# Seven block products for the gate, token scales computed one stage earlier, and gated tiles in older tiles' homes

## The chip, the cores and the metric

The kernel runs on one core of a Trainium2 chip. The time is the device time of that core for one launch, in microseconds (us). Three runs of the kernel before took 1465.34, 1465.96 and 1466.18 us; their median is 1465.96 us. The core has a matmul engine (TensorE, PE in the profile, with its weight loads in a row of their own, PEld), three engines for elementwise work (VectorE is DVE, ScalarE is ACT, GpSimd is POOL) and an engine that only issues transfers here (SyncE, SP). Each engine works through its own queue in order; semaphores tie the queues together.

## The reference

The inputs have 8 batches of 576 tokens, 4608 in all, with 8 heads of 64 features (512 features a token). Three stages follow one another. The first is an attention by 32 landmarks per head. The second transforms its output x by a real Fourier transform over tokens and features, normalizes, and runs a feed-forward pair. The third is a gated feed-forward with a shift by one token:

```
u = x + real(fft(fft(x, axis=1), axis=2));  un = normalize(u)
y = u + relu(un @ w_ch1) @ w_ch2                      # 512 -> 2048 -> 512
y_prev = y shifted by one token inside its batch (zeros at the first)
xk = mu_k * y + (1 - mu_k) * y_prev
xr = mu_r * y + (1 - mu_r) * y_prev
k  = relu(xk @ w_k);  v = (k * k) @ w_v               # 512 -> 1024 -> 512
out = sigmoid(xr @ w_r) * v                           # w_r is 512 x 512
```

## The kernel before

The 4608 tokens are cut into 9 blocks of 512. Every product of the two feed-forward stages is taken in 16-bit halves: each operand is a high and a low part, and three matmuls (high by high, high by low, low by high, the list `PARTS`) make one product. The attention and the transform of the 8 batches run beside the first blocks of the feed-forward stage. Then come, for each block, a half block `first` of the hidden layer (function `first`, results in banks `ph`) and the second layer (`second`, results in banks `acc`).

Matrices can be multiplied in 2 by 2 blocks with seven products in place of eight. `first` of the feed-forward stage does so from block 3 on, and `first` of the gated stage does so for `w_k`: the operand is turned into seven sums and differences of its blocks (`split` in `prep`, 128 by 512 elements each), the weights likewise (`pair` in the background), and the seven products of 12 matmuls with 256 columns are added up in two banks, with copies by ScalarE and additions by VectorE in between. The gate, `xr @ w_r`, is taken plainly before: `gate(j)` makes 12 matmuls with 512 columns for each of four token groups, in a bank `gp` of its own, and one Sigmoid.

`prep(i)` makes the operands of gated block i. It loads the block and the token before it (`yb`), squares the four feature quarters on ScalarE, adds them on GpSimd, transposes and sums them (`token_sums`: 4 transposes and a reduction), turns the sum of each token into powers of two (`r`, `nz`, `qi`), spreads `r` over the partitions (`spread`: 4 transposes into a bank), copies that to `rs`, and then, for each quarter and each of the two mixes, runs one ScalarE and two VectorE instructions (`mixed`). `xk` is split into seven parts, `xr` into four, each with one ScalarE copy (high part) and one GpSimd subtraction (low part).

What is recorded is put in order by a planner (`Plan.issue`, with costs from `Engine.cost` and a priority `lead`), except the matmuls with `chain=True`: these keep the order in which the program records them. `fillers` lays that order: between the steps of `first` stand one or two pieces of the previous half block's `second` and of the gate. So TensorE's order is fixed by hand, and the other engines' by the planner.

Of the eight banks, `acc` holds 0 to 3 and `ph` 4 and 5; everything named `gp` shares the last two. Memory is cut into pools: `com` lives throughout; `pa` (with `ub`, `w2`, `uc`, `un` and `w1`) ends with the feed-forward stage, and what is in `pb2` (for blocks 1 to 8 everything that `prep` makes, `k2`, `sg`, the second half of `w_v`) starts only when the last use of anything in `pa` is over. `pb` starts when the attention's pools are done.

In the profile L190 is the recorder of every VectorE, ScalarE and GpSimd instruction, L335 is `mm`, L351 is `tr` (transposes) and L319 is every transfer. So the tile names tell the operations apart: `gp<-w_r,xr` is the gate, `ph<-xk,w_k` the hidden layer, `acc<-w_v,k` the second layer of the gated stage, `rm` a product's copy, `k` a square of the hidden layer (`k2` in the code).

Of the kernel before, what the change touches and what calls it, by code (L numbers as in the profile page):

```python
# [23 lines left out]
DM = H * D  # L24
# [172 lines left out]
class Plan:  # L197
# [28 lines left out]
    def tile(self, pool, shape, dt, name, tag=None, bufs=1):  # L226
# [12 lines left out]
        return Ref(t, view)  # L239

# [829 lines left out]
def build(nc, tc, a):  # L1070
# [5 lines left out]
    with stack, tc.manual_schedule():  # L1076
# [53 lines left out]
        def rows_of(name, r, g):  # L1130
# [3 lines left out]
            "w_k": [128, 2, 7, 2, FF2 // 2], "w_r": [128, 2, 4, DM],  # L1134
# [24 lines left out]
        def w2_room():  # L1159
            return iss.tile(pa, [128, 2, 4, DM], F16, "w2", bufs=3)  # L1160
# [7 lines left out]
        far_pairs = [far_pair("w_k", c, g) for g in range(2) for c in range(2)]  # L1168
        far_items = [
            (rows_of("w_v", r, 0), kept[f"w_v{r // 4}"][:, :, r % 4]) for r in range(8)  # L1170
        ] + [(rows_of("w_r", r, 0), kept["w_r"][:, :, r]) for r in range(4)]
# [131 lines left out]

        ORDER = [4 * g + f for g in range(4) for f in (2, 3, 0, 1)]
# [16 lines left out]
        def copy(ps, func=AF.Copy):  # L1321
            t = room()
            s_.activation(t, ps, func)
            return t

        class Block:
# [78 lines left out]
            def second(self, f, half):  # L1405
# [21 lines left out]
                for m in (2 * half, 2 * half + 1):  # L1427
# [3 lines left out]
                    iss.load(ys[:, m, BLK * self.i:BLK * self.i + BLK], u[m])  # L1431

# [6 lines left out]
        more = iss.place(pa, [128, 2, 2 * WCH + 2], I32, "more", "ub_2")  # L1439
# [85 lines left out]
        for n in ("w_k", "w_r", "w_v0"):  # L1525
            fetch(pb, n)
# [7 lines left out]
        fetch(pb2, "w_v1")  # L1534

        def prep(i):
            iss.lead = SOON
            pool, nb = (pb2, 2) if i else (pb, 1)
# [6 lines left out]
            q = None  # L1545
            for c in range(0, 4, 2):
                pair = []
                for d in (c, c + 1):
                    pair.append(
                        iss.tile(com, [128, BLK + 1], F32, "sq", "h", 3) if i  # L1550
                        else iss.tile(pool, [128, BLK + 1], F32, "sq", bufs=3)
                    )
                    s_.activation(pair[-1], y[:, d], AF.Square)
                g_.tensor_tensor(pair[1], pair[0], pair[1], op=ALU.add)
                if q is not None:
                    g_.tensor_tensor(pair[1], pair[1], q, op=ALU.add)
                q = pair[1]
            o = D * i
            s2 = tmp("s2")
            g_.tensor_tensor(s2, q[:, 1:], q[:, 0:BLK], op=ALU.add)  # L1560
            if i < B:
                g_.tensor_copy(s2[:, o:o + 1], q[:, o + 1:o + 2])
            ss = token_sums(s2)
            ex = small().bitcast(I32)
            v_.tensor_scalar(
                ex, ss.bitcast(I32), 24, None, op0=ALU.logical_shift_right
            )
            r, ri = small(), small()
            v_.tensor_scalar(r.bitcast(I32), ex, -1, 196, op0=ALU.mult, op1=ALU.add)
            v_.tensor_scalar(  # L1570
                r.bitcast(I32), r.bitcast(I32), 23, None, op0=ALU.logical_shift_left
            )
            v_.tensor_scalar(ri.bitcast(I32), ex, 58, None, op0=ALU.add)
            v_.tensor_scalar(
                ri.bitcast(I32), ri.bitcast(I32), 23, None, op0=ALU.logical_shift_left
            )
            nz, qi = [iss.tile(com, [128, 4], F32, n, bufs=3) for n in ("nz", "qi")]
            v_.tensor_scalar(nz, ri, 1.0 / WS, None, op0=ALU.mult)
            v_.scalar_tensor_tensor(qi, ri, 0.25, ri, op0=ALU.mult, op1=ALU.mult)
            rb = spread(r)  # L1580
# [147 lines left out]
        def fillers(n):  # L1728
# [6 lines left out]
            if i == NB:  # L1735
                return late
# [109 lines left out]
```

## Time and profile before

| What | Value |
|---|---|
| median of three runs | 1465.96 us |
| the profiled execution, device time | 1466.6 us |
| its span, first to last instruction | 1464.8 us |
| TensorE busy | 1441.8 us (98%) |
| VectorE, ScalarE, GpSimd busy | 995.1, 695.9, 368.4 us (68%, 48%, 25%) |
| mean granted clock of TensorE | 0.994 of full speed |
| gated stage, first `ph<-xk,w_k` to last `acc<-w_v,k` | 999.4 to 1460.2 us |

The page's chain of work that ended last is 95% TensorE. A matmul's busy time there overlaps its neighbour's, so its mean in the grouped lines (379 ns for 512 columns) is a latency and not what one more of it costs; what one costs is read from the chain of work, where a run of x12 or x24 matmuls has the time it took from start to next start. Idle time of VectorE, ScalarE and GpSimd counts only where TensorE waits for them.

### The profile page before, as it was taken

The page shows a single profiled execution, that of the slowest core. Times are in us where ns is not written, and L with a number is a line of the kernel's source. Part 1 is how long each engine was busy: PE and PEld are TensorE (multiplying, and loading weights), DVE is VectorE, ACT ScalarE, POOL GpSimd, SP SyncE. Part 2 cuts the span into 40 slices and gives each one's busy share as a digit, 9 for nine tenths or more (in the row PEclk, how much of TensorE's full clock was granted, in tenths as well). Part 3 has the DMA queues.
Part 4 walks back from the last instruction along what each step waited for, and adds up shares of the span by engine and source line. Part 5 has one row for each costly group of instructions (what it writes and reads, how often), then busy time and mean ns, then how long its engine had stood idle before and what let it go on. Part 6 is the DMA issues. An engine that isn't in the chain of part 4 may idle for free.

```text
span 1464.8 us, 25189 instructions
## 1 busy us (share of the span) xinstructions
PE 1441.8 (98%) x10016; PEld 878.7 (60%) x10016; DVE 995.1 (68%) x1976; ACT 695.9 (48%) x1430; POOL 368.4 (25%) x429
## 2 busy tenths in 40 slices
PE   9889999999999999999999999999899999999998
PEld 5445445554566676666666666666566666666664
DVE  7877685765865786776767685324687788768762
ACT  4776544454453444454554533224545545454531
POOL 3012123232320123031022121001434434353410
PEclk9989999999999999999999999999999999999999
DMA  8695663634735545555466663412001110101000
GB/s 309 203 333 201 218 216 101 233 134 151 251 128 190 202 153 184 200 195 179 145 220 239 260 221 131 158 59 87 29 30 58 37 51 29 58 30 55 34 30 29
DMA packets 76790, 211.40 MB, mean 144 GB/s; under 512 B 6400, under 2 KB 31232, under 8 KB 66816
## 3 DMA queue, kind: packets, MB, share of 16 engines
q1 hardware_dynamic: 76672, 209.78, 40.8%
q8 instruction: 79, 1.29, 0.4%
q14 instruction: 39, 0.32, 0.1%
HBM read 168.34 MB, written 41.42 MB: 143 GB/s over the span
## 4 chain that ended last, share of the span: by engine, by line
PE 95%; DVE 3%; ACT 1%; DMA 0%; POOL 0%; issue 0%; DVEq 0%; ACTq 0%; POOLq 0%
PE acc L335 38%; PE ph L335 35%; PE gp L335 18%; PE gp L351 3%; PE spare L1122 1%; DVE uc L190 0%; DMA more<-in_w_ch 0%; DVE un L190 0%; DVE small L190 0%; POOL xk L190 0%; DVE A L190 0%; ACT Y L190 0%; DVE mx L190 0%; DVE w L190 0%; DVE cst L190 0%
## 5 line engine op out<-in xcount | busy, mean ns | idle before, releaser
L335 PEld LDWEIGHTS <-w 128*128 128x128 f16 x4320 | 417.7, 99 | 298.7 <-issue 41.7
L335 PE MATMUL acc<-h,w 128*128 128x512 f16 x1728 | 429.2, 380 | 3.3 <-DVE A L190 3.3
L335 PE MATMUL ph<-un,w 128*128 128x256 f16 (+1 forms) x2592 | 405.1, 298 | 3.5 <-DVE un L190 1.9
L190 DVE TENSOR_TENSOR rm<-ph,rm 128x512 f32<-128x512 f32 x126 | 86.9, 689 | 184.9 <-ACT rm L190 130.9
L335 PE MATMUL acc<-w_v,k 128*128 128x512 f16 x864 | 199.2, 380 | 0.0
L335 PE MATMUL ph<-xk,w_k 128*128 128x256 f16 x1512 | 184.1, 275 | 5.0 <-POOL xk L190 2.2
L190 ACT ACTIVATE rm<-ph 128x512 f32<-128x512 f32 x144 | 85.9, 597 | 197.7 <-PE ph L335 196.7
L335 PEld LDWEIGHTS <-w_k 128*128 128x128 f16 x1512 | 149.1, 99 | 42.0 <-issue 6.0
L335 PEld LDWEIGHTS <-k 128*128 128x128 f16 x864 | 84.7, 98 | 86.4 <-issue 0.5
L190 POOL TENSOR_TENSOR xk<-xt,xk 128x512 f16<-128x512 f32 x63 | 85.4, 1366 | 139.3 <-ACT xk L190 138.7
L335 PE MATMUL gp<-w_r,xr 128*128 128x512 f16 x432 | 99.3, 379 | 0.3 <-POOL xr L190 0.3
L190 ACT ACTIVATE k<-rm 128x512 f16<-128x512 f32 x72 | 44.9, 627 | 85.4 <-DVE rm L190 85.3
L190 ACT ACTIVATE h<-ph 128x512 f16<-128x512 f32 x72 | 42.9, 595 | 88.7 <-PE ph L335 88.6
L190 DVE SCALAR_TENSOR_TENSOR h<-ph,h 128x512 f16<-128x512 f32 x72 | 49.4, 686 | 44.0 <-ACT h L190 43.8
L190 ACT ACTIVATE h<-rm 128x512 f16<-128x512 f32 x72 | 45.2, 628 | 65.6 <-DVE rm L190 64.5
L190 POOL TENSOR_TENSOR sq<-sq 128x513 f32<-128x513 f32 x27 | 37.9, 1403 | 151.3 <-ACT sq L190 150.5
L190 DVE SCALAR_TENSOR_TENSOR rm<-rm 128x512 f32<-128x512 f32 x72 | 71.2, 1001 | 3.9 <-ACT rm L190 2.9
L335 PEld LDWEIGHTS <-xr 128*128 128x128 f16 x432 | 42.2, 98 | 47.5 <-POOL xr L190 0.8
L190 DVE SCALAR_TENSOR_TENSOR xt<-yb,mus,xt 128x512 f32<-128x512 f32 x72 | 60.6, 876 | 12.9 <-POOL xt L190 7.2
L190 POOL TENSOR_TENSOR xr<-xt,xr 128x512 f16<-128x512 f32 x36 | 46.4, 1304 | 81.9 <-ACT xr L190 81.9
L190 DVE SCALAR_TENSOR_TENSOR h<-rm,h 128x512 f16<-128x512 f32 x72 | 53.1, 739 | 10.3 <-ACT h L190 9.7
L190 DVE TENSOR_TENSOR xt<-xt,rs 128x512 f32<-128x512 f32 x72 | 56.7, 828 | 3.0 <-ACT rs L190 2.9
(169 smaller groups left out, 1945.2 us busy)
## 6 DMA issues: line engine op xcount, KB each, us to landing
w<-dw SPq DMA_DIRECT2D x24, 1792.0 KB, 7.3
w<-dw SPq DMA_DIRECT2D x32, 1024.0 KB, 8.8
wst<-in_w_ch SPq DMA_DIRECT2D x36, 512.0 KB, 4.5
q<-in_q SPq DMA_DIRECT2D x16, 578.0 KB, 5.5
k<-in_k SPq DMA_DIRECT2D x16, 576.0 KB, 5.1
ys<-ub SPq DMA_DIRECT2D x36, 256.0 KB, 3.9
out<-o SPq DMA_DIRECT2D x36, 256.0 KB, 2.1
yb<-ys SPq DMA_DIRECT2D x8, 1026.0 KB, 5.2
```

Of the source, the lines that this page charges most:

```text
L190: f(real(out), *map(real, args), **{k: real(x) for k, x in kw.items()})
L335: self.nc.tensor.matmul(out.real(), lhsT=lhsT.real(), rhs=rhs.real(), start=start, stop=stop, **kw)
L351: self.nc.tensor.transpose(out.real(), in_.real(), ident.real())
L1122: nc.tensor.matmul(into.real() if into else spare[0], lhsT=z.to_broadcast([128, 128]), rhs=z.to_broadcast([128, 512]), start=not into, sto ...
```

## The change

Six things are done at once.

1. The gate is taken in seven block products, as `w_k` is. `w_r` is parked as seven combinations (`[128, 2, 7, 2, 256]`), `xr` is split into seven parts. `gate` is a generator of seven steps of 12 matmuls with 256 columns. All seven use one bank in turn; three partial results are copied by ScalarE to tiles `gm`, and later added to the bank by VectorE. The Sigmoids take 256 columns each.
2. The gate's steps all stand in the first half of a block, and the pieces of `second` are halved and laid anew (`fillers`).
3. The token scales `r`, `nz`, `qi` are made in the feed-forward stage, as soon as a block's result `u` is there (function `scales`, called from the end of `second`), and kept for all nine blocks. `prep` only spreads `r`, and VectorE reads it from the bank instead of from the copy `rs`.
4. The hidden layer's relu and square, one VectorE instruction before, are ScalarE instructions now (Relu, then Square; for one of four results the Relu is in the copy already).
5. `ub` and `w2` move from `pa` to `com`. In the gated stage their three homes each take `k2` (`ub_0`, `ub_1`), the halves of `w_v` (`w2_0`, `w2_1`) and `sg` (`ub_2`, `w2_2`), by a new function `spot`. The output product is written into `sg` itself instead of a tile `o`.
6. `xk` and `xr` have one tile in `pb` (even blocks) and one in `pb2` (odd blocks).

The core of the diff:

```diff
+    def spot(self, pool, shape, dt, name, place):
+        self.turn[pool, place] = 0
+        self.slots[pool, place + "_0"] = self.slots.pop((pool, place), None)
+        x = self.tile(pool, shape, dt, name, place)
...
-                u = iss.tile(pa, [128, 4, BLK], F32, "ub", bufs=3)
+                u = iss.tile(com, [128, 4, BLK], F32, "ub", bufs=3)
...
+        far_pairs += [far_pair("w_r", c, 0) for c in range(2)]
...
+        def scales(i, u):
+            iss.lead = SOON
+            q = iss.tile(com, [128, BLK + 1], F32, "q")
...
+            for c in (0, 2):
+                x, z = tmp("sq"), tmp("sq")
+                s_.activation(x, u[c], AF.Square)
+                s_.activation(z, u[c + 1], AF.Square)
+                g_.tensor_tensor(z, x, z, op=ALU.add)
+                sums.append(z)
+            g_.tensor_tensor(q[:, 1:], *sums, op=ALU.add)
...
+            ss = token_sums(s2)
...
+            kept_scales.append((r, nz, qi))
...
+                if half:
+                    scales(self.i, u)
...
-        fetch(pb2, "w_v1")
+        for n in range(2):
+            x = f"w_v{n}"
+            ws[x] = iss.spot(com, shapes[x], F16, x, f"w2_{n}")
+            iss.load(ws[x], kept[x])
...
-            rb = spread(r)
-            rs = tmp("rs")
-            s_.activation(rs, rb, AF.Copy)
+            rs = spread(r)
...
-            def gate(self, j):
+            def gate(self):
                 iss.lead = NOW
+                sg = iss.spot(com, [128, 2, 2, DM], F32, "sg", "ub_2" if self.i % 2 else "w2_2")
...
+                def run(ps, w, b, opens):
+                    for j in range(2):
+                        for c in range(2):
+                            for n, (x, y) in enumerate(PARTS):
+                                mm(
+                                    ps[:, HB * j:HB * j + HB],
+                                    self.xr[y][:, b, c, 128 * j:128 * j + 128],
+                                    wr[x][:, w, c], opens and j == 0 and c == 0 and n == 0,
...
                 ps = gp()[0]
+                run(ps, 0, 0, True)
+                copy(ps, t=t1)
+                yield
+                run(ps, 4, 5, False)
+                copy(ps, t=t2)
+                yield
+                run(ps, 5, 6, False)
+                copy(ps, t=t3)
+                yield
+                run(ps, 2, 3, False)
+                out(ps, 1, 0)
+                yield
+                run(ps, 3, 4, True)
+                v_.tensor_tensor(t3, ps, t3, op=ALU.add)
+                out(t3, 1, 1)
+                yield
+                run(ps, 6, 2, False)
+                v_.tensor_tensor(t2, ps, t2, op=ALU.add)
+                out(t2, 0, 1)
+                yield
+                run(ps, 1, 1, True)
+                v_.tensor_tensor(t1, ps, t1, op=ALU.add)
+                out(t1, 0, 0)
+                yield
...
-                    v_.scalar_tensor_tensor(t, t, 0.0, t, op0=ALU.max, op1=ALU.mult)
+                    if relu:
+                        s_.activation(t, t, AF.Relu)
+                    s_.activation(t, t, AF.Square)
...
-                    o = iss.tile(pb2, [128, 512], F32, "o", bufs=3)
+                    o = self.sg[j]
...
             if i == NB:
-                return late
-            gates = [partial(blocks[i].gate, 2 * g + j) for j in range(2)]
-            return gates if not late else late[0:2] + gates[0:1] + late[2:4] + gates[1:2]
+                return [late]
+            if g:
+                return [late[0:1], late[1:3], late[3:5], late[5:6], late[6:7], late[7:8]]
+            steps = blocks[i].gate()
+            gates = [partial(next, steps) for _ in range(7)]
+            return [[*late[k:k + 1], gates[k], *(late[7:8] if k == 6 else [])] for k in range(7)]
```

Three places show what the planner makes of it. The first is SyncE's queue where the gated stage begins. `w_517` and `w_519` are block 8's last first-layer weights, `w_10495` and `w_10731` its second-layer weights, `ys<-ub` its results, `yb<-ys` with 513 columns the input of gated block 1 (then of block 2), and `w_v` the gated stage's second matrix. Before:

```order
L319 DMA w_517<-dw_3_82 128x7168
L319 DMA w_10495<-dw_3_90 128x4096
L319 DMA ys<-ub 128x512 x4
L319 DMA yb<-ys 128x4x513
L319 DMA w_v_10908<-dw_v_78 128x4096
L319 DMA yb<-ys 128x4x513
L319 DMA out<-o 128x512 x4
```

Now:

```order
L328 DMA w_519<-dw_3_82 128x7168
L328 DMA w_10731<-dw_3_90 128x4096
L328 DMA w_v_10934<-dw_v_77 128x4096
L328 DMA yb<-ys 128x4x513
L328 DMA w_v_11104<-dw_v_78 128x4096
L328 DMA ys<-ub 128x512 x4
L328 DMA yb<-ys 128x4x513 x2
L328 DMA out<-sg 128x512 x4
```

Block 1's input is now loaded ahead of the feed-forward stage's last results, not behind them; block 2's follows at once, and both halves of `w_v` stand here.

The second place is ScalarE's queue at the start of gated block 0. `rm<-ph` are copies of the hidden layer's products, `sq` the squares for token scales, `xt` the mixes of block 1, `k_10985` the block's squared hidden layer. Before:

```order
L190 ACTIVATE rm<-ph 128x512
L190 ACT_TABLE_LOAD
L190 ACTIVATE sg<-gp,nz 128x512
L190 ACTIVATE rm<-ph 128x512
L190 ACTIVATE sg<-gp,nz 128x512
L190 ACTIVATE rm<-ph 128x512
L190 ACTIVATE sq<-yb 128x513 x3
L190 ACTIVATE rm<-ph 128x512
L190 ACTIVATE k_10985<-rm 128x2x256
L190 ACTIVATE xt_10994<-yb,mus 128x512
```

Now, from the copy of the gate's third product to the Sigmoids of its fifth (`rm<-rm` are Relu and Square, `k_11357` the squared hidden layer, `gm` the gate's partial results):

```order
L190 ACTIVATE gm<-gp 128x512
L190 ACTIVATE rm<-rm 128x512
L190 ACTIVATE rm<-ph 128x512
L190 ACTIVATE rm<-rm 128x512
L190 ACTIVATE k_11357<-rm 128x2x256
L190 ACTIVATE rm<-rm 128x512
L190 ACTIVATE k_11357<-rm 128x2x256
L190 ACT_TABLE_LOAD
L190 ACTIVATE sg<-gp,nz 128x256 x2
L190 ACTIVATE rm<-rm 128x512 x4
L190 ACTIVATE k_11357<-rm 128x2x256 x2
L190 ACTIVATE sg<-gm,nz 128x256 x2
```

The mixes and squares have left this place; the table load and the first Sigmoids stand behind six instructions on the hidden layer, and six more stand before the next Sigmoids.

The third place is VectorE's queue at the end of block 0's first half, where the gate's last three products of that block stand (`gm<-gp,gm` is the addition that empties the gate's bank, `rm<-ph,rm` that of the hidden layer). Before:

```order
L190 TENSOR_TENSOR rm<-ph,rm 128x512
L190 SCALAR_TENSOR_TENSOR k_10985<-rm,k_10985 128x2x256
L190 SCALAR_TENSOR_TENSOR rm<-rm 128x512 x2
L190 SCALAR_TENSOR_TENSOR k_10985<-rm,k_10985 128x2x256
L190 SCALAR_TENSOR_TENSOR xt_10994<-yb,mus,xt_10994 128x512
L190 SCALAR_TENSOR_TENSOR k_10985<-rm,k_10985 128x2x256
```

Now:

```order
L190 TENSOR_TENSOR rm<-ph,rm 128x512
L190 TENSOR_TENSOR xt<-xt 128x2x256
L190 TENSOR_TENSOR xt_11128<-xt_11153,xt_11128 128x2x256
L190 TENSOR_TENSOR gm<-gp,gm 128x512
L190 TENSOR_TENSOR xt<-xt 128x2x256
L190 SCALAR_TENSOR_TENSOR k_11357<-rm,k_11357 128x2x256 x2
L190 TENSOR_TENSOR gm<-gp,gm 128x512
L190 TENSOR_REDUCE small<-gp 128x4
L190 TENSOR_SCALAR small<-small 128x4
L190 TENSOR_SCALAR r<-small 128x4
L190 TENSOR_TENSOR gm<-gp,gm 128x512
```

Between the first and the second `gm` addition stand two instructions that need ScalarE's last two `k_11357`.

## Rows read from the trace of the kernel before

**Rows 1.** Windows: stretch, length, busy us of each engine, granted clock, DMA.
```profile
850.00:999.36 149.36, 149.36 (x990) 96.72 (x988) 68.30 (x114) 42.39 (x71) 13.46 (x13) 1.00 0.35 131
1055.00:1065.00 10.00, 7.15 (x32) 4.31 (x31) 4.39 (x10) 8.28 (x14) 5.09 (x7) 0.66 0.01 2
1066.40:1449.81 383.41, 383.41 (x2434) 238.95 (x2433) 280.86 (x397) 180.24 (x309) 141.72 (x152) 1.00 0.11 39
```

**Rows 2.** TensorE's groups from 960 us on: form, count, busy us, idle before.
```profile
L335 PE MATMUL acc<-w_v,k 128*128 128x512 f16 x864 | 199.2, 380 | 0.0
L335 PE MATMUL ph<-xk,w_k 128*128 128x256 f16 x1512 | 184.1, 275 | 5.0 <-POOL xk L190 2.2 <-ACT xk L190 2.0 <-ACT rm L190 0.7
L335 PE MATMUL gp<-w_r,xr 128*128 128x512 f16 x432 | 99.3, 379 | 0.3 <-POOL xr L190 0.3
```

**Rows 3.** Chain of work, the gated stage's start and an undisturbed stretch: start us, us, what.
```profile
999.36 2.62 PE ph L335 x24
...
1109.05 2.59 PE gp L335 x12
1111.64 2.62 PE ph L335 x24
...
1118.60 2.59 PE acc L335 x12
...
1125.96 0.44 PE gp L351 x4
```

**Rows 4.** Timeline of the end: start us, us, engine, what, [idle before, releaser].
```profile
1455.69 4.48 PE L335 MATMUL acc<-w_v,k 128*128 128x512 f16 x20
...
1461.20 0.75 DVE L190 SCALAR_TENSOR_TENSOR o<-acc,qi,sg 128x512 f32<-128x512 f32 x1 [0.87 <-DMA out<-o]
```

**Rows 5.** TensorE's timeline, where it waits: start us, us, [idle before, releaser].
```profile
1010.52 6.71 PE L335 MATMUL ph<-xk,w_k 128*128 128x256 f16 x60 [0.74 <-ACT rm L190]
...
1043.13 1.36 PE L335 MATMUL ph<-xk,w_k 128*128 128x256 f16 x11 [1.38 <-POOL xk L190]
...
1054.74 0.60 PE L335 MATMUL gp<-w_r,xr 128*128 128x512 f16 x2 [0.28 <-POOL xr L190]
1057.33 0.37 PE L335 MATMUL ph<-xk,w_k 128*128 128x256 f16 x1 [1.99 <-ACT xk L190]
1058.56 5.07 PE L335 MATMUL ph<-xk,w_k 128*128 128x256 f16 x23 [0.86 <-POOL xk L190]
```

**Rows 6.** Timelines of SyncE, TensorE and ScalarE: block 1's operands.
```profile
1004.26 0.58 SPq L319 DMA_DIRECT2D yb<-ys  x1
...
1024.32 0.60 PE L351 MATMUL gp<-ident,small 128*128 128x128 f32 x4
...
1056.66 0.62 ACT L190 ACTIVATE xk<-xt 128x512 f16<-128x512 f32 x1
```

**Rows 7.** ScalarE's timeline: table load and first Sigmoid.
```profile
1004.23 1.28 ACT L190 ACT_TABLE_LOAD   x1 [2.94 <-DMA ys<-ub]
1005.53 0.69 ACT L190 ACTIVATE sg<-gp,nz 128x512 f32<-128x512 f32 x1
```

**Rows 8.** ScalarE and VectorE groups: form, count, busy us, mean ns, idle before.
```profile
L190 ACT ACTIVATE sq<-yb 128x513 f32<-128x513 f32 x32 | 19.0, 624 | 1.5 <-DMA yb<-ys 1.5
L190 ACT ACTIVATE sg<-gp,nz 128x512 f32<-128x512 f32 x36 | 24.6, 684 | 40.5 <-PE gp L335 40.3 <-DVE qi L190 0.2
L190 ACT ACTIVATE Ae<-d 97x256 f16<-97x256 f32 x24 | 9.8, 408 | 0.1
L190 DVE SCALAR_TENSOR_TENSOR rm<-rm 128x512 f32<-128x512 f32 x72 | 71.2, 1001 | 3.9 <-ACT rm L190 2.9
```

**Rows 9.** VectorE by tile: duration ns min/median/max, first and last start us.
```profile
L190 DVE TENSOR_TENSOR rm<-ph,rm x126: 675/691/693, 440.3 to 1444.7; 128x512 f32<-128x512 f32 x126
L190 DVE SCALAR_TENSOR_TENSOR k<-rm,k x72: 673/683/1764, 1014.1 to 1446.8; 128x512 f16<-128x512 f32 x72
L190 DVE TENSOR_TENSOR xt<-xt,rs x72: 677/684/1660, 860.6 to 1402.1; 128x512 f32<-128x512 f32 x72
```

More of the change, by code (lines that the diff above doesn't have):

```diff
@@ L239, in tile @@
         return Ref(t, view)
+    def spot(self, pool, shape, dt, name, place):
+        self.turn[pool, place] = 0
+        self.slots[pool, place + "_0"] = self.slots.pop((pool, place), None)
+        x = self.tile(pool, shape, dt, name, place)
+        x.tile.make = lambda: pool.get().tile(list(shape), dt, tag=place, name=name, bufs=1)
+        self.slots[pool, place] = self.slots.pop((pool, place + "_0"))
+        return x
     def place(self, pool, shape, dt, name, place):
@@ L1319, in room, with copy @@
             return iss.tile(com, [128, 512], F32, "rm", bufs=5)
-        def copy(ps, func=AF.Copy):
-            t = room()
+        def copy(ps, func=AF.Copy, t=None):
+            t = t or room()
             s_.activation(t, ps, func)
@@ L1436, in halves @@
                 ]
-        more = iss.place(pa, [128, 2, 2 * WCH + 2], I32, "more", "ub_2")
+        more = iss.place(com, [128, 2, 2 * WCH + 2], I32, "more", "ub_2")
         rooms = [None, None, more[:, 0], more[:, 1]]
@@ L1523, in fetch @@
             iss.load(ws[n], kept[n])
[L1525 removed]
+        for n in ("w_k", "w_r"):
             fetch(pb, n)
@@ L1544, in prep @@
                 iss.load(y, ys[:, :, BLK * i - 1:BLK * i + BLK])
[L1545 to L1557, printed above, removed]
@@ L1570, in prep @@
[L1570 to L1579, printed above, removed]
@@ L1655, in first @@
                 xk = self.xk
-                k2 = iss.tile(pb2, [128, 2, 4, BLK], F16, "k2", bufs=2)
+                k2 = iss.spot(com, [128, 2, 4, BLK], F16, "k2", f"ub_{g}")
                 self.ks[g] = k2
@@ L1701, in first, with second @@
                 yield
-            def second(self, f):
+            def second(self, f, half):
                 iss.lead = NOW
-                if f == self.order[0]:
+                if f == self.order[0] and half == 0:
                     self.acc = acc_banks()
@@ L1708, in second @@
                 opens, closes = f == self.order[0], f == self.order[-1]
-                for j in range(4):
+                js = (2 * half, 2 * half + 1)
+                for j in js:
                     sl = slice(128 * j, 128 * j + 128)
@@ L1733, in fillers @@
                 u, p = divmod(n - 1, 2)
-                late = [partial(blocks[u].second, f) for f in Gated.order[4 * p:4 * p + 4]]
+                late = [
+                    partial(blocks[u].second, f, k)
+                    for f in Gated.order[4 * p:4 * p + 4] for k in range(2)
+                ]
             if i == NB:
-                return late
-            gates = [partial(blocks[i].gate, 2 * g + j) for j in range(2)]
-            return gates if not late else late[0:2] + gates[0:1] + late[2:4] + gates[1:2]
+                return [late]
[4 more added lines that the diff above has]
+            return [[*late[k:k + 1], gates[k], *(late[7:8] if k == 6 else [])] for k in range(7)]
         blocks = {}
```

152 lines of the change are left out of this document (88 added, 64 removed).

## The prediction

> **What bounds the kernel now.** I read the windows first. In the undisturbed part of the gated stage TensorE is busy 383.41 of 383.41 us, VectorE 73%, ScalarE 47%, GpSimd 37% of it [rows 1]; the reader is to see that only TensorE's own work, and what makes it wait, counts. The same holds for the end of the feed-forward stage, 149.36 of 149.36 us [rows 1]. So the question is how many matmul columns go, what one costs, and which waits of TensorE go or come.
>
> What one costs is read from the chain in an undisturbed stretch [rows 3]: 24 products of 256 columns take 2.62 us, 0.1092 us each; 12 of 512 columns take 2.59 us in the gate and in the second layer, 0.2158 us each; 4 transposes 0.44 us. The group line's 379 ns and its 99.3 us [rows 2] include overlap.
>
> Now the stage is added up. It holds 1512 hidden-layer products, 864 of the second layer and 432 of the gate [rows 2], and 64 transposes (8 for each of blocks 1 to 8): 165.1 + 186.5 + 93.2 + 7.0 = 451.8 us. It runs from 999.36 [rows 3] to 1455.69 + 4.48 = 1460.17 [rows 4], 460.8 us. So 9.0 us are lost, and TensorE's timeline says where: idle 0.74, 1.38, 0.28, 1.99 and 0.86 us, all between 1009 and 1059 [rows 5], 5.25 together, then 23 products in 5.07 us where 2.51 is their due, with the granted clock at 0.66 over ten microseconds [rows 1], its lower level for part of them. The rest is pipeline refill behind each wait and the slow tail of that stretch. After that nothing is lost.
>
> These waits are for block 1's operands. Its input is loaded at 1004.26, behind the feed-forward stage's last results; its scales are spread at 1024.32; its last hidden-layer part is copied at 1056.66 [rows 6], just when TensorE waits for it [rows 5].
>
> **The change part by part.** The gate: 7 products of 12 matmuls, 84 a block, 756 in all, of the same 256-column shape, with a weight load for each, as the hidden layer's. 756 x 0.1092 = 82.5 us against 93.2: **-10.7 us**. All of it lies on TensorE's path. I see no bound that would raise the price: the hidden layer runs at it with its own weight loads.
>
> The token scales: their 4 transposes a block move to the feed-forward stage, where TensorE is as full; moved, not saved, 0. Four squares, three additions and a sum a block move with them, to engines that had room there: VectorE 68.3, ScalarE 42.4, GpSimd 13.5 of 149.4 us [rows 1]. The planner places them anew among the attention's work; I bound what TensorE waits for that by nothing saved (it is fully busy there) and nine times the smallest wait seen in the gated stage, 0.28 us [rows 5], 2.5; I take **+0.5**.
>
> The old waits: block 1's input now stands ahead of the last feed-forward results in SyncE's queue, since pb2 no longer waits for ub and w2; its scales are long there, so the spread stands in the third product of block 0, some 5 us after the stage's start against 25 before. The 32 us from spread to last part [rows 6] then end at about 37; block 1's first product comes two half blocks after the start, 2 x 9.2 (hidden layer) + 9.2 (gate) + 10.4 (48 second-layer products) + 1 (transposes) + the new waits below, 42 us. So the last part is there some 5 us early and the 9.0 us go: **-9.0**. What would be late next are block 0's own copies.
>
> Squares on ScalarE: 72 VectorE instructions of 1.0 us go [rows 8], 126 of about 0.62 come (the square row's 0.624 [rows 8]). With three more copies of gate results, three more parts of xr, eight Sigmoids of half width for four, and without squares and rs, ScalarE gets some 10 us more a block: 47% of 50.3 us is 24, so 34 of 48.7, 70%. VectorE loses 8 x 1.0 and gains 3 additions and about 4 differences of 0.69: less busy than before. Off the path while each finds its place, and priced where it doesn't, next.
>
> Block 0's first half has no second-layer pieces to stand between the gate's steps, and its last three gate products stand with nothing between them, all in one bank. I follow the queues shown with the change, in us from the stage's start. TensorE is through the fourth gate product at 13.5 and through the hidden layer and four transposes at 15.3. ScalarE copied the third gate product by 10.2, then has six instructions of 0.62 (14.0), the table load of 1.28 [rows 7] (15.3) and two Sigmoids. A 256-column Sigmoid isn't in the trace; it costs between the 0.408 of a 256-column copy and the 0.684 of the 512-column one [rows 8]; I take 0.45, near the first, which has its width: 16.2. The fifth product waits until then, 0.9. It ends at 17.5; the addition of 0.69 (rm<-ph,rm, [rows 9]) frees the bank at 18.3, a wait of 0.8. The sixth ends at 19.6. VectorE's next addition stands behind two k instructions that need ScalarE's four Relu and Square and two copies (16.2 + 6 x 0.62 = 19.9); with 0.68 and 0.69 it ends at 21.4, a wait of 1.8. Sum **+3.5**. Bounds: 1.5, when only the two additions are waited for, and 6.1, with Sigmoids at 0.684 and two VectorE instructions at the 1.76 maximum [rows 9].
>
> On the table load the row shows 1.28 us and the first Sigmoid 0.02 us behind it [rows 7]. The Trainium skill, "ScalarE: Activation LUTs", section "What ACT_TABLE_LOAD costs", adds a drain of about 1.38 us to each load. By that rule the fifth product would wait 1.4 us longer and the time would be 1451.8 in place of 1450.4; no drain shows in the row, and I leave it out.
>
> In blocks 1 to 8 the fifth and sixth products each have six second-layer matmuls behind them, 1.29 us, in which VectorE must add and free the bank. With an instruction of median length just begun that is 0.68 + 0.69 = 1.37, a wait of 0.08; with one at the maximum 1.16 [rows 9]. 16 places: between 0 and 18.6 us; I take **+1.0**, near the median.
>
> Reading the spread scales from the bank eight times, not from the copy: the addition with a bank operand takes 0.691 and at most 0.693, the multiplication by rs 0.684 and up to 1.66 [rows 9]. So 0, with less stretching. The Trainium skill, "VectorE: DVE Perf Modes", section "Rules for kernel authors", says to copy a bank out first where many operations read it. By that rule the copy should have stayed; the rows make eight reads dearer by 0.06 us together, and neither is on TensorE's path.
>
> The end: the last output product waits 0.87 us for a transfer to free its tile [rows 4]. In sg's own place it doesn't: **-0.9**. The remaining moves of tiles cost nothing that I can find: the homes of k2, sg and w_v fall free before the feed-forward stage's last results are stored, except sg's first, which the last second-layer matmuls read and which is written 13 us later.
>
> Sum against the profiled execution: 1466.6 - 10.7 - 9.0 - 0.9 + 3.5 + 1.0 + 0.5 = 1451.0 us. That execution lies 0.6 above the median of the runs shown, so I say **1450.4 us**.
>
> **The rivals.** (a) The clock falls behind block 0's three waits. For it: before, 3.1 us of idle within 4 us brought it down; the single wait of 1.38 did not [rows 5]. Here it is 3.5 within 8. Price from the same rows, 5.07 - 2.51 and the slow tail, 3.0: 1453.4 us.
> (b) Block 1's operands are late all the same, because ScalarE, at 70%, gives their copies away to block 0's: 9.0 us stay. Against it: a lead of 20 us in the spread. 1450.4 + 9.0 = 1459.4 us.
> (c) No new waits at all, the planner's order holding exactly: 1450.4 - 5.0 = 1445.4 us.
> (d) Slower: the gate's single bank. In blocks 1 to 8 VectorE comes to the two additions behind stretched instructions every time: 16 x 1.16 - 1.0 = 17.6 more, and in half of the blocks the clock falls as in (a), 4 x 3.0: 1480 us. It decides from 18.5 us more than forecast, 1.2 us in each of the 16 places. Against it: with fewer VectorE instructions and 1.29 us of cover, the median makes 0.08.
> That the gate does not get cheaper at all is no case of its own: the shape's price stands in 1512 instances.
>
> **How the numbers follow.** Forecast 0.70, (a) 0.13, (b) 0.08, (c) 0.05, (d) 0.04. The forecast's own terms span from 1446 (waits at their lower bounds) to 1455 (block 0 at 6.1, the feed-forward stage at 2.5); (a) lies inside; (b) is taken in for the part in which some of its 9.0 us stay. Range 1446 to 1458. A measurement of this kernel can tell about 0.2%, 2.9 us, from no change: faster means below 1463.0. All but (d), and a (b) that brings other waits with it, lie below: faster 0.94, same 0.02, slower 0.04.
>
> **What would show it.** The gate's line should read 756 of 128x256, and a stretch of the chain 1.31 us for 12 of them. From the stage's first product to its last matmul I expect 1512 + 756 products of 0.1092, 864 of 0.2158, 36 transposes and 4.5 of waits: 442.6 us, against 460.8. TensorE's waits should stand in block 0 at gate products five to seven, on ScalarE's sg and VectorE's gm, not at block 1's first products on xk. The last output product should have no transfer ahead of it. The prediction is wrong if TensorE waits in every block on gm or rm, if block 1 still waits on xk, or if waits appear before the gated stage where there were none.

## The result and the profile after

The changed kernel takes 1453.21 us (median of four runs, 1451.67 to 1453.36) against 1465.65 of the kernel before beside it: 0.9913 of its time, interval 0.9896 to 0.9930. The forecast was 1450.4, the range 1446 to 1458. In a later session (the run `again` below) it took 1451.49 against 1466.03, 0.9902, interval 0.9888 to 0.9915. The profiled execution is the shortest of the four, 1451.67 us, and its span is 1449.8; the other three took 1.5 to 1.7 us more.

The windows answer to [rows 1]; a line gives the stretch, its length, the busy time of TensorE, its weight loads, VectorE, ScalarE and GpSimd, then TensorE's granted clock and the transfers. The second is the whole gated stage, the third its undisturbed part.

```profile
850.00:1003.98 153.98, 153.98 (x1020) 100.20 (x1019) 97.34 (x158) 73.36 (x123) 38.12 (x48) 1.00 0.51 188
1003.98:1445.44 441.46, 438.47 (x3168) 310.21 (x3166) 287.49 (x386) 304.03 (x541) 153.59 (x164) 1.00 0.11 39
1066.00:1432.00 366.00, 366.00 (x2639) 258.42 (x2638) 231.56 (x310) 252.20 (x450) 120.16 (x131) 1.00 0.11 38
```

TensorE's gap in the stage is 441.46 - 438.47 = 2.99 us, and from 1066 us on it has none. ScalarE is now the busiest of the three others there, 69% against VectorE's 63%; before it was 47% and 73%. The clock reads full in all three, where [rows 1] had a stretch at 0.66.

TensorE's groups from 960 us on answer to [rows 2]:

```profile
L344 PE MATMUL acc<-w_v,k 128*128 128x512 f16 x864 | 204.7, 379 | 0.0
L344 PE MATMUL ph<-xk,w_k 128*128 128x256 f16 x1512 | 180.2, 273 | 0.0
L344 PE MATMUL gp<-w_r,xr 128*128 128x256 f16 x756 | 93.1, 273 | 3.0 <-DVE gm L190 2.0 <-ACT sg L190 1.0
```

The idle time has moved from the hidden layer's products (5.0 us, on xk and rm) to the gate's (3.0 us, on gm and sg). The busy column would say that the gate fell from 99.3 to 93.1 us only; the chain, which answers to [rows 3], gives the true price:

```profile
1003.98 2.62 PE ph L344 x24
...
1088.57 0.44 PE gp L360 x4
...
1099.21 1.31 PE gp L344 x12
...
1101.83 1.29 PE acc L344 x6
...
1108.35 2.62 PE ph L344 x24
```

Twelve gate products take 1.31 us, the hidden layer's price. The three waits, in TensorE's timeline (answering to [rows 5]):

```profile
1020.24 1.47 PE L344 MATMUL gp<-w_r,xr 128*128 128x256 f16 x12 [0.98 <-ACT sg L190]
1022.49 1.47 PE L344 MATMUL gp<-w_r,xr 128*128 128x256 f16 x12 [0.78 <-DVE gm L190]
1025.19 1.47 PE L344 MATMUL gp<-w_r,xr 128*128 128x256 f16 x12 [1.23 <-DVE gm L190]
```

What stood in front of them on ScalarE, and then on VectorE:

```profile
1017.40 0.63 ACT L190 ACTIVATE k<-rm 128x512 f16<-128x512 f32 x1
1018.05 1.28 ACT L190 ACT_TABLE_LOAD   x1
1019.35 0.84 ACT L190 ACTIVATE sg<-gp,nz 128x256 f32<-128x256 f32 x2
1020.08 2.47 ACT L190 ACTIVATE rm<-rm 128x512 f32<-128x512 f32 x4
1022.58 1.15 ACT L190 ACTIVATE k<-rm 128x512 f16<-128x512 f32 x2
```

```profile
1021.75 0.69 DVE L190 TENSOR_TENSOR gm<-gp,gm 128x512 f32<-128x512 f32 x1 [0.99 <-PE gp L344]
1022.35 0.68 DVE L190 TENSOR_TENSOR xt<-xt 128x512 f32<-128x512 f32 x1
1023.24 1.29 DVE L190 SCALAR_TENSOR_TENSOR k<-rm,k 128x512 f16<-128x512 f32 x2 [0.21 <-ACT k L190]
1024.45 0.68 DVE L190 TENSOR_TENSOR gm<-gp,gm 128x512 f32<-128x512 f32 x1
```

The table load (1.28 us) lies right before the Sigmoids of the fourth product, and they start 0.02 us after it, as in [rows 7]. The seventh product's addition (1024.45) stands behind two k instructions, which stand behind ScalarE's four rm and two k.

SyncE's timeline shows the earlier load that [rows 6] is compared with: 992.35 against 1004.26 us, some 11 us ahead of the stage's start, not 5 behind it. TensorE spreads block 1's scales at 1008.29, 4.5 us after the start, and GpSimd is through with block 1's xk at 1035.89, 10 us before its first product.

```profile
974.12 0.32 SPq L328 DMA_DIRECT2D w_v<-dw_v  x1
992.35 0.57 SPq L328 DMA_DIRECT2D yb<-ys  x1
...
1008.29 0.60 PE L360 MATMUL gp<-ident,r 128*128 128x128 f32 x4
...
1030.04 5.85 POOL L190 TENSOR_TENSOR xk<-xt,xk 128x512 f16<-128x512 f32 x4
...
1046.03 2.78 PE L344 MATMUL ph<-xk,w_k 128*128 128x256 f16 x24
```

The end, against [rows 4], with the time that the last transfer takes from issue to landing:

```profile
1440.75 4.70 PE L344 MATMUL acc<-w_v,k 128*128 128x512 f16 x21
1443.54 2.73 DVE L190 SCALAR_TENSOR_TENSOR sg<-acc,qi,sg 128x512 f32<-128x512 f32 x4 [7.61 <-PE acc L344]
1444.36 2.27 SPq L328 DMA_DIRECT2D out<-sg  x4
...
DMA to landing us min/median/max: 2.1/2.1/2.1
```

The fourth output product follows the third at once. From the last matmul (1445.45) to the landing of the last transfer (1448.44) it is 3.0 us, before 3.8; to the end of the span 4.4 us, before 4.7.

### The profile page after: what moved, and what is told of

It reads as the page before. It is cut to its first block, busy times and chain, and to the rows that moved or that the text cites. A ratio compares the mean times of both kernels' runs of the same rounds, so it can differ in the third digit from the quotient of the medians.

```text
span 1449.8 us, 26141 instructions
## 1 busy us (share of the span) xinstructions
PE 1428.7 (99%) x10340; PEld 910.0 (63%) x10340; DVE 976.9 (67%) x1971; ACT 808.7 (56%) x1641; POOL 405.3 (28%) x481
## 4 chain that ended last, share of the span: by engine, by line
PE 95%; DVE 3%; ACT 1%; issue 0%; POOL 0%; DVEq 0%; ACTq 0%; POOLq 0%
PE acc L344 39%; PE ph L344 35%; PE gp L344 18%; PE gp L360 3%; PE spare L1131 1%; DVE small L190 0%; DVE uc L190 0%; ACT rm L190 0%; DVE un L190 0%; DVE A L190 0%; ACT Y L190 0%; DVE mx L190 0%; DVE cst L190 0%; DVE sm L190 0%; ACT E L190 0%
## 5 line engine op out<-in xcount | busy, mean ns | idle before, releaser
L344 PE MATMUL acc<-w_v,k 128*128 128x512 f16 x864 | 204.7, 379 | 0.0
L344 PE MATMUL ph<-xk,w_k 128*128 128x256 f16 x1512 | 180.2, 273 | 0.0
L190 POOL TENSOR_TENSOR xr<-xt,xr 128x512 f16<-128x512 f32 x63 | 80.5, 1292 | 87.4 <-ACT xr L190 71.6
L344 PE MATMUL gp<-w_r,xr 128*128 128x256 f16 x756 | 93.1, 273 | 3.0 <-DVE gm L190 2.0
L344 PEld LDWEIGHTS <-xr 128*128 128x128 f16 x756 | 74.0, 98 | 23.9 <-issue 3.5
L190 ACT ACTIVATE rm<-rm 128x512 f32<-128x512 f32 x126 | 78.5, 626 | 11.9 <-DVE rm L190 9.0
L190 DVE SCALAR_TENSOR_TENSOR k<-rm,k 128x512 f16<-128x512 f32 x72 | 52.5, 739 | 25.9 <-ACT k L190 25.7
L190 DVE SCALAR_TENSOR_TENSOR xt<-yb,mus,xt 128x512 f32<-128x512 f32 x72 | 55.9, 818 | 13.0 <-POOL xt L190 12.8
L190 DVE TENSOR_TENSOR xt<-xt 128x512 f32<-128x512 f32 x52 | 54.0, 1049 | 11.8 <-POOL xk L190 5.8
L190 POOL TENSOR_TENSOR wst<-wst 128x256 f32<-128x256 f32 x56 | 44.7, 818 | 47.9 <-DVE wst L190 46.7
```

The lines of the kernel that those rows point to most:

```text
L190: f(real(out), *map(real, args), **{k: real(x) for k, x in kw.items()})
L344: self.nc.tensor.matmul(out.real(), lhsT=lhsT.real(), rhs=rhs.real(), start=start, stop=stop, **kw)
```

## The experiments

All are the changed kernel with an edit, each timed against the kernel before on the same chip. Four of them (gate_plain_rs, prep_scales, late_both, dve_square) ran on another chip than the rest; across the two, the ratios to the kernel before are the safer comparison. Stage times run from the first `ph<-xk,w_k` to the last matmul of each profile; the changed kernel's is 441.6 us, that of the kernel before 461.0.

**again**: no edit.

> The changed kernel once more, unaltered. Its first four runs lay at 1451.7 (the profiled one) and at 1453.1 to 1453.4, spans 1449.8 and 1451.3 to 1451.5. Theory 1, that the 1.6 us between them are TensorE's clock after block 0's three waits (2.99 us idle within 6 us), expects runs at both levels again, and in a profile of a longer run a stretch of granted clock below 1 right behind 1026 us that is not there in the first profile. Theory 2, that they come from the attention's start or from transfers, expects the difference elsewhere in the span and block 0 alike in both.

1451.49 us (1451.02 to 1453.32), stage 441.6, waits of 1.0 and 2.0 us as before. Both levels came again, but the profile is of a shorter run, so theory 1 was not tested by it directly. Against theory 1 speaks gate_spread below: without any wait in block 0 its runs spread just as much, 1447.91 to 1449.96. For theory 2 speak the windows from 50 to 100 us. TensorE's instructions come in the same order there in all these kernels, and still the windows differ; in the changed kernel's profile, in that of `again` and in that of prep_scales (below) they read

```profile
50.00:100.00 50.00, 42.11 (x318) 21.15 (x304) 41.46 (x100) 37.98 (x73) 3.34 (x4) 0.93 0.80 272
```
```profile
50.00:100.00 50.00, 42.85 (x304) 21.66 (x303) 42.24 (x100) 37.22 (x72) 2.88 (x4) 0.90 0.80 273
```
```profile
50.00:100.00 50.00, 45.50 (x328) 23.12 (x321) 39.78 (x93) 37.03 (x72) 2.89 (x4) 0.86 0.76 254
```

The granted clock (third number from the end) is 0.93, 0.90 and 0.86 there, with TensorE's busy time longer the lower it is. The first two differ by little in time: the gated stage starts at 1003.8 and, at the lower clock, at 1003.5. The third costs more. spread_prep (below) has TensorE's instructions in the same order as prep_scales up to the gated stage, and 0.93 in this window; the same matmuls stand 2.4 us apart just behind it, first in spread_prep, then in prep_scales, and the stage starts 2.4 us apart too (999.1 and 1001.5):

```profile
100.61 1.92 PE L344 MATMUL acc<-h,w 128*128 128x512 f16 x6 [3.34 <-DVE A L190]
```
```profile
102.97 2.74 PE L344 MATMUL acc<-h,w 128*128 128x512 f16 x6 [3.34 <-DVE A L190]
```

So a difference of the size in question does arise in the first 100 us. That a given run's 1.6 us came from there is not shown, since none of the longer runs has a profile.

**gate_plain**: the gate as before, all else as changed.

```diff
-                run(ps, 0, 0, True)          # seven steps in one bank
-                copy(ps, t=t1)
...
+                for k in range(7):
+                    if k % 2 == 0:           # four products, 12 matmuls of 512 columns
+                        ps = gp()[0]
...
+                        s_.activation(self.sg[j], ps, AF.Sigmoid, scale=self.nz[:, j:j + 1])
+                    yield
```

> The changed kernel with the gate taken plainly again: four products of 12 matmuls with 512 columns in each first half block, each in a bank of its own, one Sigmoid each; xr in four parts, w_r as before; all else as changed. If the gate's columns are the gain, the gated stage gets 10.7 us longer (432 x 0.2158 against 756 x 0.1092) and loses block 0's three waits (3.0 us and what the clock takes): 1452 to 1453 + 7.7 = 1459 to 1461 us, and chain pieces of 2.59 us for 12 gate products. If the gain were the earlier operands alone, it stays within 2 us of the changed kernel.

1463.89 us, stage 454.6: more than expected. Block 0 waited for something new (first TensorE's timeline, then VectorE's, then the window behind 1016 us):

```profile
1011.52 1.47 PE L344 MATMUL ph<-xk,w_k 128*128 128x256 f16 x12 [0.69 <-ACT rm L190]
1012.83 0.60 PE L360 MATMUL gp<-ident,s 128*128 128x128 f32 x4
1016.66 4.23 PE L344 MATMUL gp<-w_r,xr 128*128 128x512 f16 x12 [3.23 <-DVE xt L190]
```
```profile
1009.88 4.26 DVE L190 TENSOR_TENSOR xt<-xt,gp 128x512 f32<-128x512 f32 x7
...
1015.93 0.68 DVE L190 TENSOR_TENSOR xt<-xt,gp 128x512 f32<-128x512 f32 x1
```
```profile
1016.25:1019.66 3.41, 3.00 (x8) 1.08 (x9) 3.41 (x4) 3.38 (x7) 3.41 (x3) 0.50 0.00 0
```

Twelve matmuls that take 2.59 us elsewhere took 4.23; the granted clock reads 0.50, the lower of its two levels, from 1016.25 to 1019.66. A plain gate product needs a fresh bank. The four transposes of a token sum had taken one of the two at 1012.83, and VectorE's eight multiplications by the spread scales were still reading the other: the last ends at 1016.61, and the product starts 0.05 us later. So in block 0's first half the direct read of the scales' bank and a plain gate get in each other's way. With the plain gate in the second half (plain_spread, below) TensorE waits for no bank of the gate.

**gate_plain_rs**: gate_plain with `rs` copied out again.

```diff
-            rs = spread(r)
+            rb = spread(r)
+            rs = tmp("rs")
+            s_.activation(rs, rb, AF.Copy)
```

> gate_plain with the spread scales copied out of their bank again (one ScalarE copy, VectorE multiplies by the copy). gate_plain took 1463.9 us and waited 3.23 us for a bank in block 0, since a plain gate needs a new bank for each product and VectorE's eight multiplications held one of the two. If that is the reason, this wait goes, with the clock's loss behind it, and what is left of the difference to the changed kernel is the gate's columns, 10.7 us, less the changed kernel's own three waits of 3.0: 1451.5 + 7.7 = 1459 us. If the waits stay, the plain gate is late for another reason, and the time is 1462 to 1464.

1488.87 us: neither. The planner laid block 0 differently. TensorE waited 5.47 us for a scales' sum, and the stage started at 1013.6 (1003.7 in gate_plain); in it TensorE waited for the copy itself, and the stage took 470.2 us:

```profile
1034.67 4.69 PE L344 MATMUL gp<-w_r,xr 128*128 128x512 f16 x12 [11.40 <-ACT rs L190]
```

It tells nothing of the gate's columns, and that gate_plain's 3.23 us were the bank's remains a reading of its profile. The copy alone was not put back into the changed kernel, so what the direct read is worth there is not shown.

**gate_spread**: block 0's last three gate products in its second half.

```diff
+        self_steps = []
...
+            if i == 0:
+                if g == 0:
+                    self_steps.append(blocks[0].gate())
+                x = [partial(next, self_steps[0]) for _ in range(4 if g == 0 else 3)]
+                if g == 0:
+                    return [[y] for y in x]
+                return [
+                    [late[0], x[0]], late[1:3], [late[3], late[4], x[1]], late[5:6],
+                    [late[6], x[2]], late[7:8],
+                ]
```

> The changed kernel with block 0's last three gate products moved from its first half, where nothing stands between them, into its second half, among the second layer's pieces; all else alike. If the three waits of 0.98, 0.78 and 1.23 us are the bank's, they go and nothing takes their place: 3.0 us less than the changed kernel's best, 1448.7, and if they also cost the clock in some runs, 4.5 less than its median, with all runs within 0.5 us. If instead ScalarE's queue in block 0 is what is late, the waits move to the hidden layer's copies and the time stays within 1 us.

1448.38 us, 3.1 less than `again` beside it; stage 438.4, 3.2 less; TensorE waits for nothing in it. The window that held the three waits (47.01 of 50.00 us busy in the changed kernel) is full:

```profile
1000.00:1050.00 50.00, 50.00 (x386) 37.62 (x384) 40.00 (x51) 42.43 (x76) 25.70 (x31) 1.00 0.13 45
```

So the three waits were the bank's, with nothing behind them. Run again beside the last three experiments:

> gate_spread once more, to stand beside the three others on the same chip: 1448 to 1449 us, no wait of TensorE in the gated stage; what differs between its runs should lie in the first 150 us, where the granted clock differs from run to run.

1449.32 us (1448.08 to 1450.17), stage 438.4. The first profile of gate_spread has a clock of 0.90 from 50 to 100 us, this one 0.93, and the stages start at 1003.3 and 1004.0 us; so the spread of its runs isn't pinned on the clock in that stretch.

**plain_spread**: gate_spread with the plain gate of gate_plain, block 0's four products in its second half.

> gate_spread (no wait left in block 0) with the gate taken plainly again: block 0's four gate products of 12 matmuls with 512 columns stand in its second half, later blocks' in the first half, each in a new bank. Neither kernel should wait in block 0, so the difference is the gate's columns alone: 432 x 0.2158 against 756 x 0.1092, 10.7 us. gate_spread's gated stage took 438.4 us; this one's should take 449.1, and the whole 1448.4 + 10.7 = 1459 us. If the seven products were cheaper or dearer than 0.1092 us a matmul, the stage says so: each 0.01 us is 7.6 us.

1459.56 us, stage 450.1, with 0.94 us of waits on rm in block 0:

```profile
1007.46 1.47 PE L344 MATMUL ph<-xk,w_k 128*128 128x256 f16 x12 [0.25 <-ACT rm L190]
1009.61 2.78 PE L344 MATMUL ph<-xk,w_k 128*128 128x256 f16 x24 [0.69 <-ACT rm L190]
```

450.1 - 438.4 - 0.94 = 10.8 us: the gate's columns, measured by themselves.

**late_pool**: pb2 waits for the last use of ub and w2.

```diff
+        ff = blocks
...
-        pb2 = Pool(stack, tc, "pb2", (pa_stack,), iss.fence(pa), side="right")
+        held = {x[0].tile for x in ub.values()} | {w.tile for x in ff for w in x.w2s}
+        ends = iss.fence(pa)
+        for t in held:
+            for e in ends:
+                e.preds.update(o for o in t.ops if o.eng not in ("s", None))
+        pb2 = Pool(stack, tc, "pb2", (pa_stack,), ends, side="right")
```

> The changed kernel with one thing undone: the pool pb2 waits for the last use of ub and w2 again, though nothing of it lies there. Block 1's input is then loaded behind the feed-forward stage's last results, some 15 us later. If the old waits went because of the earlier pool, part of the 9.0 us of the kernel before come back, on xk or xr of block 1 between 1040 and 1065 us: 1457 to 1463 us. If the lighter prep (no squares, no token sums) alone did it, the time stays at 1452 to 1454 and TensorE waits nowhere in block 1.

1456.73 us, 5.2 more than `again`, just under the expected span. The stage, 445.3, is 3.7 us longer; the rest lies ahead of it (in the two profiles it starts at 1005.5 and 1003.5). Waits on xk of block 1 are back, 3.3 us:

```profile
1049.48 1.36 PE L344 MATMUL ph<-xk,w_k 128*128 128x256 f16 x11 [0.53 <-POOL xk L190]
...
1056.34 1.36 PE L344 MATMUL ph<-xk,w_k 128*128 128x256 f16 x11 [2.78 <-POOL xk L190]
```

**prep_scales**: the scales made in `prep`, from the loaded block.

```diff
-                if half:
-                    scales(self.i, u)
...
+            scales(i, [y[:, c, 1:] for c in range(4)])
             r, nz, qi = kept_scales[i]
```

> The changed kernel with the token scales made in prep alone undone; the pool still starts early. The 28 transposes return to the gated stage, 0 in sum. If the earlier pool alone is enough, block 1's operands stay in time and the kernel takes 1451 to 1453 us. If the 20 us of lead come mainly from the scales, waits on xk appear in block 1 as in late_pool: 1455 to 1458.

1450.35 us, a little under the expected span, ratio 0.9891 against 0.9902 of `again`: no loss. The stage is 3.0 us longer (28 transposes come to 3.1) and starts earlier; block 1 doesn't wait.

**late_both**: late_pool and prep_scales together.

> The changed kernel with two things undone: pb2 waits for ub and w2 again, and the token scales are made in prep, from the loaded block, as before. late_pool alone cost 5.2 us of the 9.0 that the old waits took. If the scales' early place is worth the rest, this kernel loses about 9 us on the changed one, 1460 to 1461 us, with waits of 4 to 6 us on xk of block 1. If the scales don't matter, it stays at late_pool's 1456 to 1457.

1464.91 us, 13.4 more than `again` (12.3 by the ratios, 0.9986 against 0.9902), worse than expected: 3.65 and 4.36 us on xk, three more waits on gm in later blocks (1.13, 0.37 and 0.33 us), and a granted clock of 0.91 from 1050 to 1100 us.

```profile
1048.86 0.37 PE L344 MATMUL ph<-xk,w_k 128*128 128x256 f16 x1 [3.65 <-ACT xk L190]
1053.60 2.50 PE L344 MATMUL ph<-xk,w_k 128*128 128x256 f16 x11 [4.36 <-POOL xk L190]
```

The four kernels answer together. The stage, less the 3.1 us of transposes where it holds them, takes 441.6 us with pool and scales early, 441.6 with the pool alone early (prep_scales), 445.3 with the scales alone early (late_pool) and 455.4 with neither. So the early pool by itself removes all the old waits, and the early scales help only where the pool is late; there they save 10.1 of 13.8 us.

In late_both, block 1's input is asked for at 1002.70, but its first squares stand behind block 0's hidden-layer instructions and Sigmoids in ScalarE's queue, 18.5 us later; in the kernel before it was 6.1 us (1004.26 to 1010.37). First late_both's ScalarE, then that of the kernel before:

```profile
1021.24 1.13 ACT L190 ACTIVATE sq<-yb 128x512 f32<-128x512 f32 x2
```
```profile
1010.37 1.66 ACT L190 ACTIVATE sq<-yb 128x513 f32<-128x513 f32 x3
```

**dve_square**: relu and square as one VectorE instruction again.

```diff
-                    if relu:
-                        s_.activation(t, t, AF.Relu)
-                    s_.activation(t, t, AF.Square)
+                    v_.scalar_tensor_tensor(t, t, 0.0, t, op0=ALU.max, op1=ALU.mult)
```

> The changed kernel with the hidden layer's relu and square as one VectorE instruction again. If ScalarE's queue makes block 0's fifth and seventh gate products wait, these two (0.98 and 1.23 us) shrink and VectorE, at 65% in the changed kernel, has room for 72 more instructions: 1449 to 1451.5 us. If moving the squares was needed, VectorE comes late to the gate's additions in every block: waits on gm in blocks 1 to 8 of up to 1.2 us each and 1455 us or more.

1452.09 us (1450.18 to 1452.50), just over the expected span, stage 440.7. The fifth product's wait fell from 0.98 to 0.30, the seventh's from 1.23 to 0.93, and nothing else waited. Moving the squares was not needed: within what these runs can tell, it neither gains nor costs here.

**spread_prep** and **spread_prep_dve**: gate_spread with the scales in `prep`; the second with VectorE's squares too.

> gate_spread with the token scales made in prep again, as in prep_scales. With the pool early, prep_scales lost nothing by that (its waits before the gated stage were 0.6 us fewer). Then this kernel takes 1447.5 to 1448.5 us, the gated stage 3.1 us longer (28 transposes) and the stretch before it as much shorter. If the scales' early place helps once block 0 runs without waits, 1450 us or more and waits on xk in block 1.

1447.46 us, 0.988 of before, interval 0.9867 to 0.9892; gate_spread_2 beside it 1449.32, 0.9889. Waits of 1.1 us on gm in blocks 2 and 3.

> spread_prep with relu and square as one VectorE instruction again. dve_square cost nothing and took block 0's waits from 2.99 to 2.01 us; with these waits gone anyway the two should be the same within 1 us: 1447 to 1449 us. If ScalarE's share of the work is what keeps block 1's operands in time when the squares for the scales are there as well, waits on xk or gm appear with VectorE at over 80%: 1450 us or more.

1450.06 us: 2.6 more than spread_prep (its stage, 445.2 against 442.8, is 2.4 longer), with six waits of some 0.25 us for ScalarE's gm copies and 0.7 us on xk. Where prep also makes the scales, the squares on ScalarE pay a little.

gate_spread and spread_prep are faster than both given kernels: their runs lie between 1447.12 and 1450.17 us, all below the shortest of the changed kernel's (1451.02), although the intervals of the ratios touch. Between these two the intervals overlap.

## Why the prediction was right

The sum forecast 15.6 us off the profiled execution; the two profiles differ by 14.9 (1466.6 to 1451.67), the medians by 12.4 and, in the later session, 14.5. The other three runs of the first session, 1.5 to 1.7 us above the profiled one, are outside the sum, and their cause stays open. Term by term:

- **The gate**, -10.7: measured by itself, 10.8 (plain_spread against gate_spread).
- **The old waits**, -9.0: all gone, and TensorE waits for no xk. The cause was the one named, the earlier pool (prep_scales and late_both, which differ in it alone). What the prediction gave as its second half, the scales being ready, was not needed (prep_scales): the early load alone gave lead enough. The spread came 4.5 us after the stage's start, for 5, and block 1's first product at 42.2, for 42. The last part of xk was there at 32, for 37, so the lead was twice the one forecast.
- **Block 0's waits**, +3.5: 2.99 of idle time, 3.2 by the stages of the changed kernel and gate_spread, in the places and by the releasers named: 0.98, 0.78 and 1.23 for 0.9, 0.8 and 1.8. The third was overstated, though the addition that it waits for ended when forecast (21.3 us after the stage's start, for 21.4): the sixth product ended at 20.1, not at 19.6, so less was left to wait for. Half-width Sigmoids last 0.46 to 0.51 us where 0.45 was taken.
- **Blocks 1 to 8**, +1.0: no wait in the changed kernel. In 15 of the 16 places VectorE begins the addition 0.04 us after the product has ended, once 0.26 us after it, and it is through 0.19 to 0.40 us before the next product; no stretched instruction stood in front of it.
- **The feed-forward stage**, +0.5: mis-sized. The gated stage starts 4.6 us later, 3.1 of them transposes; 1.5 remain. TensorE's visible idle time between 205 and 980 us went from 0.5 to 1.0 us, the rest isn't pinned to a wait. The profiles of prep_scales and spread_prep, with the scales away from there, show only the old 0.5 us. New are 0.29 us before `gp<-k,qbd` at 361.5 and 0.16 us twice on ScalarE's Y, at 529.4 and 753.9. The prediction had named waits in this place as a sign that it is wrong; they came, but only in the size of its own term.
- **The end**, -0.9: the wait for a transfer went, and the last output lands 3.0 us after the last matmul, before 3.8, so this part came as forecast. But from that landing to the end of the span it is 1.4 us, before 0.8, and -0.3 is left of the term. The last transfer itself takes as long as before, 2.1 us for 2.0. Behind the last landing gate_plain, with the same output tiles, takes 0.8 us and prep_scales 1.1; what sets this time is not shown.

The three new idle times of TensorE ahead of the gated stage:

```profile
361.52 0.70 PE L344 MATMUL gp<-k,qbd 64*32 64x320 f32 x2 [0.29 <-issue]
529.35 0.33 PE L360 MATMUL gp<-ident,Y 128*128 128x128 f32 x1 [0.16 <-ACT Y L190]
753.94 0.33 PE L360 MATMUL gp<-ident,Y 128*128 128x128 f32 x1 [0.16 <-ACT Y L190]
```

The mechanism held in the large terms. That the sum came within 0.7 us of the profile's difference is partly luck: the 1.0 us counted too many for blocks 1 to 8 and the 0.3 to 0.5 for block 0 stand against 1.0 not counted in the feed-forward stage and 0.6 not counted at the end.

Rival (a), the clock falling behind block 0's waits, did not come in either profile of the changed kernel: 2.99 us idle within 6 us left it full. The prediction had read [rows 5] as 3.1 us of idle before the fall, but the clock there reads 0.50, its lower level, already from 1057.37, ahead of the last 0.86: 0.28 and 1.99 us came before. In gate_plain it reads so from 1016.25, within the wait of 3.23, and in late_both from 1048.88, behind 3.65; in late_pool it stayed full behind a single wait of 2.78. So the idle time alone does not tell these cases apart.

Rival (b) was the nearest danger, and by the mechanism named, ScalarE's queue: with the pool late, and worse with the scales late too, the lighter VectorE work doesn't save block 1. In late_both, whose squares for block 1 stand behind block 0's instructions, TensorE waits 8.0 us on xk, 4.5 on xk and xr before the change. That the squares and relus moved to ScalarE are to blame is not shown: late_both was not run with them on VectorE. Rival (d) shows only in traces, as the 0.17 to 0.72 us on VectorE's gm in spread_prep, late_pool and late_both.

The drain that the Trainium skill ("ScalarE: Activation LUTs", section "What ACT_TABLE_LOAD costs") adds to a table load was not there: the load starts 0.02 us after the instruction before it, and the next Sigmoid 0.02 us after the load, with TensorE waiting on it. Nor did eight reads of the scales' bank cost time in VectorE (a median of 680 ns, for 684 from the copy); in gate_plain they cost a bank.

## What to carry to other kernels

Price a matmul from the chain's runs of equal ones, not from the mean of its group, and then ask which bank each new product waits for: a chain of products through one bank needs other work between them, as block 0 and gate_spread show, and where none stands, each wait can be read off the order of the engines that empty the bank. When a stage starts late, look first at which pool its operands' loads wait for; giving two long-lived tiles another pool was worth more here than taking work out of the preparation. An operand read straight from a bank holds that bank until the last of its readers is through, and these may stand far apart in their engine's queue (1009.88 to 1016.61 in gate_plain). And where an experiment undoes one of two remedies, undo both as well: late_pool alone made the early pool look worth 3.7 us of the stage; with the scales late as well it is worth 13.8.

## What the runs showed that was not expected

TensorE's granted clock from 50 to 100 us lay between 0.86 and 0.93 from profile to profile (0.90 and 0.93 for the same program), although its instructions come in the same order there. Among the kernels with the scales in the feed-forward stage the gated stage starts anywhere between 1002.7 and 1005.7 us (1013.6 in gate_plain_rs, where TensorE waits just ahead of it); so differences of 2 us in whole times need the stage's own time beside them. And one more ScalarE copy (gate_plain_rs) cost 25 us, with block 0 laid in another order by the planner: an isolated edit under a planner isn't an isolated cause.
